# DRAM copies of q and k in pieces of 512 columns, fewer W2 splits in the last key blocks, first casts on two engines

## The chip, the cores and the metric

The kernel runs on one core of one Trainium2 chip. The metric is the device time of one execution, in microseconds (us). The engines are TensorE (PE), VectorE (DVE), ScalarE (ACT), GpSimd (POOL) and SyncE (SP), whose only work here is to issue DMAs.

## What is computed

For x of 2048 tokens by 512 features, all in float32:

```python
g = sigmoid((x * gate_w).sum(-1))                 # one gate for a token
qkv = x @ wqkv                                    # 32 heads of 16
scores = q @ k.T / 4, for keys within the last 256 tokens, causal
a = (softmax(scores) @ v) @ wo
y = layernorm(x)
b = gelu(y @ w1 + b1) @ w2 + b2                   # 512 -> 1792 -> 512
out = g * a + (1 - g) * b
```

## The kernel before, in words

Float32 products are made of fp32r parts: an operand is cast to a high part (`copy` on ACT, or a copy on DVE) and the rest is a low part (`lo_part`, a subtraction on DVE or POOL); three matmuls, high by high, high by low and low by high, stand for one. `split(w, raw)` makes both parts of a weight tile; with `both=True` DVE makes the high part too.

The work has three stages, and the order of the instructions on each engine is written by hand (manual schedule). A step counter helps: `after(k, fn)` puts work off to the k-th `tick()` from now, and `settle()` runs the ticks until nothing is left.

**Stage 1, QKV** (to about 154 us). x comes in four chunks of 512 tokens (`load_x`), each in four pieces by feature. `qk_unit(g, t, c)` makes q or k (t) of eight heads (g) for one chunk with 12 matmuls (L233), and writes high and low parts to DRAM tiles `qkd[g, t]` of 50 rows for a head. `v_unit` makes v for 128 tokens (L254). Where group g is 0 the high part is written twice, into rows 0 and 1 + t; for g = 1, 2, 3 `double(g)` copies it later inside DRAM (L245). `masks()` sets constants on POOL.

**Stage 2, attention and MLP1** (154 to about 527 us). Heads are taken in groups of four, p = 0 to 7, and tokens in blocks of 128. The string ORDER says what PE does next:

- S: `s_pair`, scores of one query block by its key blocks for a pair of heads (L279); DVE masks and reduces them to row maxima (L288, L289). After four query blocks `put_max` sends the maxima through DRAM (`md`) into rows of the q stacks (L307, L309).
- T: `st_pair`, transposed scores of one key block, maximum included (L323); ACT takes the exponential (L325), POOL zeroes what lies outside the window with two affine selects (L327).
- P: `pv`, probabilities by v (L342), evacuated by ACT, or by DVE once no S is left (L349), and stored to `osc` (L353).
- f: `fill`, one of the 24 steps of an `mlp1_unit` (two matmuls of 64 rows side by side, L527). There are 28 units, so 672 steps. Their result goes to DRAM, tile `hp` (L539).

A T of a new key block first calls `block(p, kb)`, which ticks, and there the loads are issued: `load_stacks` (L266) for the next p, the copies of `double`, and in the last p the W2, Wo and h tiles of stage 3. S, T and P share four double PSUM banks in turn, of which an MLP1 unit holds one. S runs ahead of T by ten query blocks (LAG is 6). All DMAs but a few go through SP, which works in order; eight semaphores are shared in turn, so an issue waits until the DMA eight before it has landed. After ORDER come the last P and the MLP1 steps that are left.

**Stage 3, MLP2 with the output projection** (527 us to the end). `mlp2(c, f)` multiplies one h tile by one W2 tile, 12 matmuls (L724), for 14 f in each of four token chunks; h tiles are loaded four steps ahead (`load_h`, L579), put through gelu on ACT (L582) and split by DVE (L586). `attn_out(c)` normalises the attention output, splits it and multiplies it by Wo (L703).

The functions that the change touches:

Of the kernel before, what the change touches and what calls it, by code (L numbers as in the profile page):

```python
# [19 lines left out]
S = 2048  # L20
D = 512
H = 32
DH = 16
F = 1792
DT = D // 128
KT = D // 64
FT = F // 128
C = 512
# [6 lines left out]
EPS = 1e-5  # L35
NEG = -3.0e38
U8 = mybir.dt.uint8
ORDER = ("fSfTffSPffTfSffTfSffTfTfffSfTffSffSfffSPSffTfSffTfSffTfffTSPSfSfTfffTfffTSfTfffSfSPSTfTSfTffffSTPSTf"
         "TffSffTfSffTPSfTfTfffSfTffSffSPSfTfffTfSfTfffSfTPTfSfTfffTfSfTffSffTSfffSPTSfTffSffTPTSffTfSfTfSffSP"
         "SfTfSffTfTfSTfffTfSfSfPTSffTfSfTfSffTPTSfTffSfTfSffTPTSfTffTffSfTffSffSPSfTSfffTfSffTfSffTfffSTPTSff"  # L40
         "TfSffTfSffffSfSPTffTfSffTfffSfTPSfTfSfffTfSffTfSffTffSffSPSTffSffTfTffSfTfffTffSPTfSfTffSfffTfSfffSP"
         "TfSfTffSfTffTfSPTfSfTffSffTfSffTfSffTffSffSPTSfTfffTfSPSffTfSffTfSffTffSffTfSffTffSffSPTSTfffSffTPTf"
         "SfTffSffTSffTfSffSPTfSfTffTfffSfSPSffTfSffTfSffTfSfffTSffTfffSTPSfTfSffTfSffSPTSfTffSffTfSffTfffTTPT"
         "fTfSffTfffTfSPTSfTffSffSPSfTSfffTfSffTffTfSfTfffTfSPSfTffSffTffSffSPTSfTfffTfSfTfffSfTPTSfTffSffTfSf"
         "fTfSffTfSffSPTSfTfffSfTfffTfSPTfSfTfffSffTfffSTPTSfTfffSfSPSffTffTfSffTffSffTfSffTfSffffSfTffSffSPSf"
         "TfffTfSfTffSffTPTfSfTffSfffTfSffTfSfffSPTfSffTfffTfSPTfSfTfffSfTffSffTfSffTffSffSPTSfTfffSfTPTfSfTff"
         "SffTfffSTPTfSffTfSffTfSfffSPTSffTfSfTfSffTfSffTSffSPTSffTfSffTffTfSfTffSfSPTfSfTffSffTTfffSPTfSffTfS"
         "ffTffTfSfffSfffSPTfSfTffSffTfSffTfSfffSPTfSfTffTffSfTfffSfSPTSTffffTSPTSfTfffTfSfTffTffSPTSfTffSffTS"
         "ffTfSffSPTSTfffSffTPTSfTffSffTSffTfSffSPSTfSTSTfTffTPTTffffTfPTfffTffTfffTffTPTffTffffTfTPTTfffffTTP"
         "TfT")  # L50
LAG = 6


# [1 line left out]
def gated_mix_kernel(ctx, tc: tile.TileContext, xt, x2, wqk, wv, wo, xa, gw, w1, w2, b1, b2, out):  # L55
# [55 lines left out]
    def view(t, *ap, off=0):  # L111
        return bass.AP(tensor=t.tensor, offset=t.offset + off, ap=[list(x) for x in ap])

    def f32(t):
        return t.bitcast(F32)

    def lo_part(lo, src, hi, eng=dve):
        eng.tensor_tensor(out=lo, in0=src, in1=f32(hi), op=ALU.subtract)  # L118

    def copy(dst, src):  # L120
        act.activation(dst, src, AF.Copy)  # L121
# [4 lines left out]
    def after(k, fn):  # L126
        todo.setdefault(step[0] + k, []).append(fn)
# [40 lines left out]
    def split(w, raw, both=False):  # L168
        if both:
            dve.tensor_copy(w[:, 0], raw)  # L170
        else:
            copy(w[:, 0], raw)
        lo_part(w[:, 1], raw, w[:, 0])

    def masks():
        for t in qs + ks:
            pool.memset(f32(t[:32]), 0.0)
        for k in ks:
            pool.memset(f32(k[96:128]), 1.0)
        one = small("scr", 2, (128, 256), BF16)  # L180
        pool.memset(one, 1.0)
        pool.affine_select(out=one[:, :128], in_=one[:, :128], pattern=[[-1, 128]], base=0, channel_multiplier=1,
                           compare_op=ALU.is_ge, fill=0.0)
# [24 lines left out]
    def load_x(c):  # L208
        h, l = x8(), x8()
        xh.append(h)  # L210
        xl.append(l)
        raw = vs[:, 4 * c:4 * c + 4].rearrange("p b r -> p (b r)")
        for dt in range(DT):
            sp.dma_start(raw[:, dt * C:(dt + 1) * C], xt[c, :, dt * C:(dt + 1) * C])

        def rest(first=None):
            for dt in range(DT):
                a, r = h[:, dt * C:(dt + 1) * C], raw[:, dt * C:(dt + 1) * C]
                copy(a, r)
# [19 lines left out]
            act.dma_start(f32(view(d, [S, DH], [50 * S, HG], [1, C], off=k * DH * S + c * C)), f32(h))  # L239
        after(1, lambda: sp.dma_start(f32(view(d, [S, DH], [50 * S, HG], [1, C], off=(2 - t) * DH * S + c * C)), f32(l)))  # L240

    def double(g):
        for t in range(2):
            fr, to = (f32(view(qkd[g, t], [S, DH], [50 * S, HG], [1, S], off=k * DH * S)) for k in (0, 1 + t))
            sp.dma_start(to, fr)  # L245

    def v_unit(b):
# [298 lines left out]
    def load_w2(f):  # L546
        if f % 2 == 0:
            w2t.append(x8())
            if f == 4:
                spare.append(x8())  # L550
        w = w2s[f] = w2t[-1][:, f % 2 * 2 * C:f % 2 * 2 * C + 2 * C].rearrange("p (k n) -> p k n", k=2)
        raw = t2()
        sp.dma_start(raw, w2[f])
        return lambda both=False: split(w, raw, both)
# [5 lines left out]
        return lambda both=False: split(w, raw, both)  # L560

    def early_w2():
        for n in range(3):
            def go(n=n):
                fns = [load_w2(2 * n), load_w2(2 * n + 1)]
                after(2, lambda: [fn(True) for fn in fns])
            after(1 + n, go)

        after(2, lambda: early_wo(0))

    def early_wo(a):
        fns = [load_wo(a), load_wo(a + 1)]
        after(3, lambda: [fn(True) for fn in fns])

    hs = {}

# [24 lines left out]
    def block(p, kb):  # L601
        tick()
        if kb % 2 == 0:
            if kb and p + 1 < 8:
                load_stacks(p + 1, kb * 128 - 256, 256)
            if not kb and p:
                load_stacks(p, S - 256, 256)
        if p in (0, 1, 3) and kb == 10:
            double((p + 3) // 2)
        if p == 7 and kb == LAG:  # L610
            early_w2()
        if p == 7 and kb == 13:
            early.extend(load_h(0, f) for f in range(4))

    early = []
# [188 lines left out]
```

## Time and profile before

| | |
|---|---|
| timed runs | 737.3 us median of 3 (733.98 to 737.37) |
| the profiled execution | 735.38 us |
| its span | 733.7 us, 16078 instructions |
| granted PE clock, mean | 0.998 |
| DMA | 138.45 MB, mean 189 GB/s |
| chain that ended last | PE 83%, DMA 6%, DVE 6%, issue 2%, ACT 1%, SP queue 1% |

The profile is of one execution. Groups of instructions give the number of them, the busy time and the mean of one. In a row of windows come the stretch, its length, and the busy time and count of PE, of its weight loads, of DVE, ACT and POOL, then PE's granted clock, the share of DMA time and GB/s. In a row of the timeline or of the chain the first number is the start and the second the duration; brackets hold the engine's idle time just before and what ended it. PE counts as busy from a matmul's start to its modelled end, so short stops between matmuls do not show as idle time. A row of the queue's waits has the sum, the number and the longest.

### The profile page before, as it was taken

Reading aid. Unit: us, or ns where it says so; the run is one execution under the profiler, and the core shown is the slowest. Engines: PE = TensorE matmul, PEld = TensorE weight load, DVE = VectorE, ACT = ScalarE, POOL = GpSimd, SP = SyncE. Lnnn points to the kernel's source line nnn. Section 1 sums busy time; section 2 is a strip of 40 time slices with the busy share of each in tenths; the row PEclk is TensorE's granted clock in tenths of the full one; section 3 lists DMA queues with packets and bytes.
Section 4 is the critical chain, followed back from the end, with each engine's and each line's share of the span. In section 5 each row is a group of like instructions: output and inputs, shape, how many; then the busy total and the mean of one; then the engine's idle time right before and its main releaser. Section 6 shows DMA issues by size and latency. Waiting matters only on the chain.

```text
span 733.7 us, 16078 instructions
## 1 busy us (share of the span) xinstructions
PE 709.5 (97%) x5728; PEld 538.7 (73%) x5728; DVE 494.8 (67%) x1049; ACT 367.7 (50%) x576; POOL 271.2 (37%) x548
## 2 busy tenths in 40 slices
PE   6999999999999899999999999999999999999997
PEld 4677777776766577777777777766678788888886
DVE  4438885778787677887778778786465645735544
ACT  4432122457667467666776767767433323223221
POOL 9220007759656355554664546547300000000000
PEclk9999999999999999999999999999999999999999
DMA  8999757776745765548664553625475544442541
GB/s 322 316 284 320 210 156 244 238 214 213 239 147 167 244 204 185 177 136 251 216 188 164 184 165 126 200 92 176 153 238 174 167 138 137 150 136 94 189 135 57
DMA packets 101795, 138.45 MB, mean 189 GB/s; under 512 B 15348, under 2 KB 54708, under 8 KB 100820
## 3 DMA queue, kind: packets, MB, share of 16 engines
q1 hardware_dynamic: 95812, 126.68, 54.5%
q10 hardware_dynamic: 5904, 10.75, 4.6%
q8 instruction: 46, 0.75, 0.4%
q14 instruction: 33, 0.27, 0.1%
HBM read 82.06 MB, written 54.28 MB: 186 GB/s over the span
## 4 chain that ended last, share of the span: by engine, by line
PE 83%; DMA 6%; DVE 6%; issue 2%; ACT 1%; SPq 1%; ACTq 0%; POOL 0%; DVEq 0%
PE ps_a L724 20%; PE ps_b L527 18%; PE ps_b L342 10%; PE ps_d L233 10%; PE ps_b L323 7%; PE ps_o L703 6%; PE ps_b L279 6%; PE ps_d L254 5%; DVE mx L289 2%; DMA v<-in_xt 1%; DVE ps_b L288 1%; DMA q<-md 1%; DMA t<-in_wo 1%; DMA t<-in_wv 1%; PE ps_x L279 1%
## 5 line engine op out<-in xcount | busy, mean ns | idle before, releaser
L327 POOL TENSOR_SCALAR_AFFINE_SELECT p<-p 128x256 f32<-128x256 f32 x480 | 186.5, 418 | 144.7 <-ACT p L325 141.8
L527 PE MATMUL ps_b<-x,w 64*128 64x512 f32 x1344 | 222.9, 395 | 0.1
L325 ACT ACTIVATE p<-ps_b 128x768 f32<-128x768 f32 (+2 forms) x256 | 191.7, 771 | 59.5 <-PE ps_b L323 52.3
L724 PE MATMUL ps_a<-x,t 128*128 128x512 f32 x624 | 149.7, 397 | 0.5 <-DVE t L586 0.5
L289 DVE TENSOR_REDUCE mx<-ps_b 128x2 f32<-128x512 f32 x208 | 144.1, 693 | 7.2
L724 PEld LDWEIGHTS ps_a<-x,t 128*128 128x128 f32 x624 | 117.2, 188 | 30.2 <-DVE t L586 1.4
L527 PEld LDWEIGHTS ps_b<-x,w 64*128 64x128 f32 x1344 | 131.8, 186 | 9.3 <-DVE t L349 0.4
L288 DVE COPY_PREDICATED ps_b<-tri,ps_b 128x256 f32<-128x256 uint8 x208 | 88.3, 424 | 50.6 <-PE ps_b L279 42.4
L233 PE MATMUL ps_d<-x,w 128*128 128x512 f32 x384 | 98.3, 407 | 8.0 <-ACT w L121 6.7
L323 PE MATMUL ps_b<-q,k 64*128 64x384 f32 (+5 forms) x512 | 97.1, 365 | 6.3 <-DVE mx L289 2.3
L342 PE MATMUL ps_b<-p,v 128*32 128x128 f32 (+1 forms) x1920 | 93.3, 332 | 0.9 <-POOL p L327 0.7
L233 PEld LDWEIGHTS ps_d<-x,w 128*128 128x128 f32 x384 | 72.6, 192 | 29.0 <-ACT w L121 6.7
L279 PE MATMUL ps_b<-k,q 62*128 62x384 f32 (+2 forms) x472 | 88.0, 352 | 3.9 <-DMA k<-qk 2.2
L342 PEld LDWEIGHTS ps_b<-p,v 128*32 128x32 f32 x1920 | 54.4, 110 | 37.0 <-issue 6.9
L323 PEld LDWEIGHTS ps_b<-q,k 50*128 50x128 f32 (+1 forms) x512 | 52.0, 184 | 38.7 <-PE ps_b L279 15.3
L121 ACT ACTIVATE t<-ps_b 128x256 f32<-128x256 f32 (+1 forms) x114 | 52.6, 489 | 51.7 <-PE ps_b L342 43.5
L279 PEld LDWEIGHTS ps_b<-k,q 62*128 62x128 f32 x472 | 48.5, 184 | 22.6 <-ACT p L325 6.0
L582 ACT ACTIVATE t<-t,b1s 128x512 f32<-128x512 f32 x56 | 38.8, 718 | 48.6 <-DMA t<-hp 48.4
L118 DVE TENSOR_TENSOR t<-t,t 128x512 fp32r<-128x512 f32 x68 | 47.1, 693 | 14.0 <-ACT t L121 11.5
L416 POOL TENSOR_TENSOR t<-t,t 128x512 f32<-128x512 f32 x16 | 22.6, 1412 | 76.8 <-DMA qk<-t 73.1
L254 PE MATMUL ps_d<-wv,x 128*128 128x512 f32 x192 | 47.5, 396 | 0.5 <-ACT wv L121 0.5
L703 PE MATMUL ps_o<-w,t 128*128 128x512 f32 x192 | 46.4, 390 | 0.0
(73 smaller groups left out, 500.7 us busy)
## 6 DMA issues: line engine op xcount, KB each, us to landing
hp<-t SPq DMA_DIRECT2D x56, 256.0 KB
t<-hp SPq DMA_DIRECT2D x56, 256.0 KB
k<-qk SPq DMA_DIRECT2D x112, 98.0 KB
q<-qk SPq DMA_DIRECT2D x112, 98.0 KB
qk<-t ACTq DMA_DIRECT2D x40, 256.0 KB
qk<-t SPq DMA_DIRECT2D x32, 256.0 KB
osc<-t SPq DMA_DIRECT2D x32, 256.0 KB
t<-in_w SPq DMA_DIRECT2D x28, 256.0 KB
```

What stands on the lines that cost most here:

```text
L233: pe.matmul(o, a[:, dt * 128:(dt + 1) * 128], b[:, dt * C:(dt + 1) * C], start=n == 0, stop=n == 11)
L254: pe.matmul(o, x[:, a:a + 128], wvs[dt][:, k], start=n == 0, stop=n == 11)
L279: pe.matmul(o[:, e, :n], qs[pr][r:k, qb * 128:qb * 128 + 128], ks[pr][r:k, t0:t0 + n], start=True, stop=True)
L288: dve.copy_predicated(o[:, :, :128], tri, o[:, :, 256:384])
L289: dve.tensor_reduce(m, o[:, :, :256], mybir.AxisListType.X, ALU.max)
L323: pe.matmul(o[:, e, :w], ks[pr][r:k, kb * 128:kb * 128 + 128], qs[pr][r:k, kb * 128:kb * 128 + w], start=True, stop=True)
L325: act.activation(pt[:, :, :w], o[:, :, :w], AF.Exp, scale=0.25)
L327: pool.affine_select(out=pt[:, :, a:a + 128], in_=pt[:, :, a:a + 128], pattern=[[0, 2], [sgn, 128]], base=b, channel_multiplier=-sgn, comp ...
L342: pe.matmul(a[32 * h:32 * h + 32, at:at + w], vs[:, kb, v:v + 32], pts[p, kb][:, h, fr:fr + w], start=n == 0, stop=n == len(parts) - 1, sk ...
L527: pe.matmul(o[:, e], w[kt // 4][r:r + 64, k, m:m + 128], y[r:r + 64, a:a + C], start=n == 0, stop=n == 23)
L703: pe.matmul(a, x[:, g], wos[g][:, k], start=n == 0, stop=n == 11)
L724: pe.matmul(accs[c][b], x[:, b * 128:(b + 1) * 128], w, start=f == 0 and n == 0, stop=f == FT - 1 and n == 2)
```

## The change

It does these things:

- The copies of `double` are made in pieces of 512 columns: two copies of 256 KB at each of key blocks 9, 11, 13 and 15 of p = 0, 1 and 3, where two copies of 1 MB stood at key block 10.
- In p = 7 four W2 tiles (one in each of four blocks) and not six W2 and two Wo tiles are loaded and split. W2 tiles 4 and 5 follow in MLP2's first steps. The Wo tiles are loaded in MLP2's first and third step and split four ticks later, with the high part on ACT and not on DVE.
- The first four h tiles are loaded at key block 12 of p = 7, not 13.
- The high part of the first weight tile is made ahead of that of the first x chunk; in the first chunk pieces 0 and 2 are cast by DVE, 1 and 3 by ACT; the low part of piece 3 is made by POOL. In all chunks the high parts are put ahead of the low parts. The clearing of 32 rows of each stack is put ahead of these casts on POOL; it was the first work of `masks()`.
- ORDER is another string: the same number of S (236), T (256) and P (64), and 655 f in place of 647, with 17 MLP1 steps left behind it in place of 25. The f are 96, 81, 80, 96, 88, 87, 86 and 41 in the eight p, after 89 (two ahead of the first T), 73, 95, 80, 85, 92, 81 and 52.

```diff
--- before.py
+++ after.py
@@ -35,19 +35,19 @@
 EPS = 1e-5
 NEG = -3.0e38
 U8 = mybir.dt.uint8
-ORDER = ("fSfTffSPffTfSffTfSffTfTfffSfTffSffSfffSPSffTfSffTfSffTfffTS
...
-         "TfT")
+ORDER = ("TSPTffffTSfTffSfSPTfSTffSfffTfSfTSffTfSfTSfSfffSPfSfTfTffff
...
+         "fTfffTPTffT")
 LAG = 6
 
 
@@ -173,8 +173,6 @@
         lo_part(w[:, 1], raw, w[:, 0])
 
     def masks():
-        for t in qs + ks:
-            pool.memset(f32(t[:32]), 0.0)
         for k in ks:
             pool.memset(f32(k[96:128]), 1.0)
         one = small("scr", 2, (128, 256), BF16)
@@ -197,6 +195,8 @@
         w, raw = wt(), t2()
         wq[g, t] = w
         (eng or sp).dma_start(raw, wqk[g, t])
+        if eng:
+            return lambda: copy(w[:, 0], raw), lambda: lo_part(w[:, 1], raw, w[:, 0])
         return lambda: split(w, raw)
 
     def load_wv(dt):
@@ -213,13 +213,16 @@
         for dt in range(DT):
             sp.dma_start(raw[:, dt * C:(dt + 1) * C], xt[c, :, dt * C:(dt + 1) * C])
 
-        def rest(first=None):
+        def part(t, dt):
+            return t[:, dt * C:(dt + 1) * C]
+
+        def rest(hi=copy, first=None):
             for dt in range(DT):
-                a, r = h[:, dt * C:(dt + 1) * C], raw[:, dt * C:(dt + 1) * C]
-                copy(a, r)
-                lo_part(l[:, dt * C:(dt + 1) * C], r, a, dve if c < 3 else pool)
-                if dt == 0 and first:
-                    first()
+                (hi if dt % 2 == 0 else copy)(part(h, dt), part(raw, dt))
+            if first:
+                first()
+            for dt in range(DT):
+                lo_part(part(l, dt), part(raw, dt), part(h, dt), dve if c and c < 3 or not c and dt < 3 else pool)
 
         return rest
 
@@ -239,9 +242,9 @@
             act.dma_start(f32(view(d, [S, DH], [50 * S, HG], [1, C], off=k * DH * S + c * C)), f32(h))
         after(1, lambda: sp.dma_start(f32(view(d, [S, DH], [50 * S, HG], [1, C], off=(2 - t) * DH * S + c * C)), f32(l)))
 
-    def double(g):
+    def double(g, c):
         for t in range(2):
-            fr, to = (f32(view(qkd[g, t], [S, DH], [50 * S, HG], [1, S], off=k * DH * S)) for k in (0, 1 + t))
+            fr, to = (f32(view(qkd[g, t], [S, DH], [50 * S, HG], [1, C], off=k * DH * S + c * C)) for k in (0, 1 + t))
             sp.dma_start(to, fr)
 
     def v_unit(b):
@@ -451,7 +454,10 @@
     x1, x2nd = load_x(1), load_x(2)
     wvr = [load_wv(dt) for dt in range(DT)]
     x3 = load_x(3)
-    x0(w0)
+    for t in qs + ks:
+        pool.memset(f32(t[:32]), 0.0)
+    w0[0]()
+    x0(dve.tensor_copy, w0[1])
     w1st()
     x1()
     masks()
@@ -546,7 +552,7 @@
     def load_w2(f):
         if f % 2 == 0:
             w2t.append(x8())
-            if f == 4:
+            if f == 2:
                 spare.append(x8())
         w = w2s[f] = w2t[-1][:, f % 2 * 2 * C:f % 2 * 2 * C + 2 * C].rearrange("p (k n) -> p k n", k=2)
         raw = t2()
@@ -560,17 +566,15 @@
         return lambda both=False: split(w, raw, both)
 
     def early_w2():
-        for n in range(3):
+        for n in range(4):
             def go(n=n):
-                fns = [load_w2(2 * n), load_w2(2 * n + 1)]
-                after(2, lambda: [fn(True) for fn in fns])
+                fn = load_w2(n)
+                after(2, lambda: fn(True))
             after(1 + n, go)
-
-        after(2, lambda: early_wo(0))
 
     def early_wo(a):
         fns = [load_wo(a), load_wo(a + 1)]
-        after(3, lambda: [fn(True) for fn in fns])
+        after(4, lambda: [fn() for fn in fns])
 
     hs = {}
 
@@ -605,11 +609,11 @@
                 load_stacks(p + 1, kb * 128 - 256, 256)
             if not kb and p:
                 load_stacks(p, S - 256, 256)
-        if p in (0, 1, 3) and kb == 10:
-            double((p + 3) // 2)
+        if p in (0, 1, 3) and kb >= NB // 2 and kb % 2:
+            double((p + 3) // 2, kb // 2 - 4)
         if p == 7 and kb == LAG:
             early_w2()
-        if p == 7 and kb == 13:
+        if p == 7 and kb == 12:
             early.extend(load_h(0, f) for f in range(4))
 
     early = []
@@ -666,7 +670,8 @@
     b2s = get("work", "b2s", 1, (128, D))
     sp.dma_start(b2s, view(b2, [0, 128], [1, D]))
 
-    early_wo(2)
+    for n in range(2):
+        after(1 + 2 * n, lambda n=n: early_wo(2 * n))
     us = {}
 
     def attn_out(c):
@@ -740,7 +745,7 @@
         for k in (n + 4,):
             c, f = item(k)
             if f >= 0:
-                if c == 0 and f > 5:
+                if c == 0 and f > 3:
                     waiting["w", f] = load_w2(f)
                 waiting[c, f] = load_h(c, f)
         c, f = item(n + 1)
```

More of the change, by code (lines that the diff above doesn't have):

```diff
@@ L37 @@
 U8 = mybir.dt.uint8
[L38 to L49, printed above, removed]
-         "TfT")
@@ new lines @@
+ORDER = ("TSPTffffTSfTffSfSPTfSTffSfffTfSfTSffTfSfTSfSfffSPfSfTfTffffTSfTfffSfSPSffTTfffSfTffTffSffSPSffTfTfff"
+         "ffSffTffSffSPSfTfSfffTfTffSfffffSffTfffTfSPTfSfTffSffSPTSffTffTfSfTffSfSPTfSfTffTffSfTfffTfSfTffSffS"
+         "PSffTSffTffTffSPTSffTffSfTffSffTPTfSffTfSffTfSffTfSffTfffSPTSTSTSPSTfSfffTffSffTfSffffTSPTfSfTfffTfS"
+         "fTffSffSPTfSffTffTfSfffTPSfTffTffSfTfffTfSfTffSffSPTSfTfffSfTffSffTPTfSfTfffSfTPSTfTfffSfTffSffSPSfT"
+         "SfffTSfffTfSfTfTffSPTSfffTSfTffTfSfTffSffSPTfSffTfSffTffTffSPTfSfTffSfffTffSfTffSffSPSfTfTfffSfTffSf"
+         "fTPTfSfTffSfffTfSffTffSffSPTfSfTffSffTfTfffSPSfTSfffTSfffTfSffTffSffSPSfTffTffSfTfffTfSPTfSfTffSffTf"
+         "fSffTfSfffSPTfSfTffTfffSPSfTfTfffSfTffSffTfSffTffSffSPTSfTfffTfSPTSfffTfSffTfSfTfSffSPTSffTffTSffTff"
+         "SPTfSfTfffTfSffTfSffTffSffSPTfSfTffSfffTffSPSTffSffTfSffTfSfffSPSfTffSffTfTffSffTfffSTPSTffTffSfTffS"
+         "ffSPTfSfTfffSfTffTffSfTfffSfSPSTfSfffTfSffTfSffTfffTSPTfSffTfSffTfSffTSffSPTfSfTffSffTffSffTPTfSfTff"
+         "TffSPTfSTfffTffSffSPTfSfTffSffTfSffTfTffSfTfffSfSPSffTfSfTfSffSPSTffTffSfTfffTfSfTffTffSPSfTfSfffTfS"
+         "fTfSffSPTfSfTffTfffSfTPSffTffSfTffSffTfSffTfSfffSPTSTfffSffTfSffTfffSTPSfTSfffTfSffTfSfffTffSPSTfSff"
+         "fTfSffTfTfSPTSfTfffSfTPTSfTffTffSfTffSffSPSTTSTSSTTPTSffTfffTTPTffTfffTfTPTTffTfffTPTfTTffffffTfPTTf"
+         "fTfffTPTffT")
```

## The prediction

> **What bounds the kernel now.** I read the page first, then the windows by stage, then the chain of waits and the timeline of TensorE around its gaps, then the queue's own waits.
>
> ```profile
> PE 709.5 (97%) x5728; PEld 538.7 (73%) x5728; DVE 494.8 (67%) x1049; ACT 367.7 (50%) x576; POOL 271.2 (37%) x548
> L289 DVE TENSOR_REDUCE mx<-ps_b 128x2 f32<-128x512 f32 x208 | 144.1, 693 | 7.2
> L288 DVE COPY_PREDICATED ps_b<-tri,ps_b 128x256 f32<-128x256 uint8 x208 | 88.3, 424 | 50.6 <-PE ps_b L279 42.4
> ```
>
> TensorE is in use for 97% of the span, so the change can gain only where PE stands still, runs at a low clock, or is held up between two short matmuls. It issues the same matmuls before and after: the letters T, S and P are the same in number in both orders, and the 672 MLP1 steps are only divided otherwise (647 in the order and 25 behind it, then 655 and 17). So I look for the places of loss.
>
> ```profile
> 154.00:203.00 49.00, 45.63 (x514) 33.69 (x514) 41.27 (x90) 33.83 (x54) 34.52 (x69) 1.00 0.71 221
> 346.00:390.00 44.00, 43.91 (x508) 33.05 (x510) 34.10 (x82) 31.45 (x48) 25.25 (x62) 1.00 0.62 190
> 481.00:521.00 40.00, 37.38 (x474) 25.14 (x470) 29.25 (x57) 26.37 (x39) 27.49 (x61) 1.00 0.42 144
> 540.00:728.00 188.00, 188.00 (x808) 151.42 (x806) 103.01 (x174) 57.53 (x90) 0.00 (x0) 1.00 0.43 138
> 253.40:257.20 3.80, 3.77 (x38) 2.19 (x40) 1.12 (x2) 1.33 (x3) 1.34 (x3) 0.55 0.46 117
> ```
>
> The first number after the stretch is its length, the second PE's busy time. From 540 to 728 us PE never rests, and from 346 to 390 it rests 0.09 us: nothing is to be had there. It rests 3.4 us at the start of attention, 2.6 us in the last head group, and in one place (253.4 to 257.2) it is busy at a granted clock of 0.55. Those, the first 40 us and the seam to MLP2 are the places where this change can act.
>
> **Prices.** From the chain of waits, back to back pieces of PE:
>
> ```profile
> 346.92 0.70 PE ps_b L527 x6
> 346.56 0.18 PE ps_b L323 x2
> 231.90 1.44 PE ps_b L342 x32
> ```
>
> So an f step (two matmuls of L527) takes 0.235 us, a T pair 0.18 us (an S pair I price alike) and a P 1.44 us. An S pair costs DVE 0.424 + 0.693 = 1.12 us.
>
> **The DRAM copies.** Before, heads' groups p = 0, 1 and 3 each issue two copies of 1 MB at key block 10. What the one in p = 1 does (first the chain, then PE's timeline, then a row of the queue's waits):
>
> ```profile
> 236.87 0.61 SPq L245
> 239.44 9.34 DMA q<-md
> 253.93 2.72 PE ps_b L342 x32
> 256.65 0.59 PE ps_b L323 x2
> ```
>
> ```profile
> 248.92 0.54 PE L323 MATMUL ps_b<-q,k 64*128 64x384 f32 x2 [0.57 <-DMA q<-md]
> 253.43 0.50 PE L279 MATMUL ps_b<-k,q 62*128 62x384 f32 x2 [2.22 <-DMA k<-qk]
> ...
> SPq L266 <- DMA qk<-qk: 13.5, 6, 2.9
> ```
>
> The copies go out at 236.87; the maxima's rows (q<-md), issued behind them at 239.44, land 9.34 us later, and the stack loads of L266 wait six times for a copy to land, 13.5 us in all: six waits for six copies. PE pays 0.57 + 2.22 us of rest, and then one P takes 2.72 instead of 1.44 us and one T pair 0.59 instead of 0.18, the low clock of the table above. Sum 0.57 + 2.22 + 1.28 + 0.41 = **4.5 us**. In p = 0 and p = 3 the same queueing costs PE nothing that I can tell: the S pairs there come later than the loads, and that lead is the cover.
>
> After, each of the three p issues eight copies of 256 KB, two at each of key blocks 9, 11, 13 and 15. SP issues 24 instead of 6: at 0.61 us each 11 us more on SP, which is spread over twelve blocks of about 2.8 us (44 us for 16 of them in the second window above). How long a 256 KB transfer keeps the queue is seen where SP waits for one landing after another:
>
> ```profile
> 536.19 0.33 SPq L553 DMA_DIRECT2D t<-in_w  x1
> 536.82 0.32 SPq L579 DMA_DIRECT2D t<-hp  x1
> 537.49 2.89 SPq L675 DMA_DIRECT2D su<-osc  x4
> ```
>
> These three issues wait for the landings of three 256 KB loads in turn: 0.63 and 0.67 us apart. A copy inside DRAM reads and writes there, so I take up to twice that, 1.3 us. Two pieces then put a load behind them back by 1.3 to 2.6 us, against the 9.34 us above. I take the whole 4.5 us as gained (0 if something else in that place is late next, which is a rival below).
>
> The rule against this edit: the Trainium skill, DMA: Bandwidth & Descriptors, section Bandwidth, says to batch DMAs to at least 1 MiB, and prices one DMA at about 2.0 us fixed plus its bytes. By that, estimated, four pieces cost 6 us more than one copy of 1 MB, and 36 us of queue over the six copies. The landings 0.67 us apart in the rows above do not bear it out for transfers in flight together. The sum goes by the rows.
>
> **The last key blocks and the splits.** Before, six W2 tiles and two Wo tiles are split on DVE alone between 505 and 516 us. The groups of that stretch, one row of the quiet stretch 346 to 390, and PE's gaps:
>
> ```profile
> L327 POOL TENSOR_SCALAR_AFFINE_SELECT p<-p 128x256 f32<-128x256 f32 x26 | 14.5, 597 | 1.4 <-ACT p L325 1.4
> L118 DVE TENSOR_TENSOR x<-t,x 128x512 fp32r<-128x512 f32 x6 | 4.6, 771 | 0.2
> L170 DVE CAST x<-t 128x512 fp32r<-128x512 f32 x6 | 3.5, 590 | 0.7 <-DMA t<-in_w 0.7
> ```
>
> ```profile
> L327 POOL TENSOR_SCALAR_AFFINE_SELECT p<-p 128x256 f32<-128x256 f32 x60 | 22.8, 408 | 20.1 <-ACT p L325 19.6
> ```
>
> ```profile
> 505.33 13.70 POOL L327 TENSOR_SCALAR_AFFINE_SELECT p<-p 128x256 f32<-128x256 f32 x24 [1.05 <-ACT p L325]
> 513.86 0.41 PE L342 MATMUL ps_b<-p,v 128*32 128x128 f32 x4 [0.71 <-POOL p L327]
> 516.64 0.50 PE L323 MATMUL ps_b<-q,k 64*128 64x256 f32 x4 [0.64 <-DVE t L349]
> ```
>
> While DVE splits, a POOL select takes 597 instead of 408 ns, and POOL works 13.7 us without a rest, so it has become the engine that the last P wait for: 26 x 0.189 = 4.9 us of POOL time. PE's visible price is 0.71 + 0.64 = 1.35 us. After, four splits (4 x 1.36 = 5.4 us of DVE, one in each block) stand for eight (10.9 us). Half of the 4.9 goes, **2.5 us**; bounds 1.35 and 4.9. The cover for the moved work is MLP2, where DVE is busy 103 of 188 us and ACT 58.
>
> **The seam to MLP2.** Two W2 splits and two Wo splits more stand in MLP2's first steps, and each transfer moved with them counts.
>
> ```profile
> 526.45 2.59 SPq L539 DMA_DIRECT2D hp<-t  x4
> 530.67 0.90 SPq L579 DMA_DIRECT2D t<-hp  x2
> 537.50 1.48 ACT L582 ACTIVATE t<-t,b1s 128x512 f32<-128x512 f32 x2 [8.82 <-DMA t<-hp]
> 538.86 6.38 PE L724 MATMUL ps_a<-x,t 128*128 128x512 f32 x25 [0.49 <-DVE t L586]
> 540.24 0.62 ACT L121 ACTIVATE x<-t 128x512 fp32r<-128x512 f32 x1
> 540.89 0.69 DVE L118 TENSOR_TENSOR x<-t,x 128x512 fp32r<-128x512 f32 x1 [0.29 <-ACT x L121]
> ```
>
> The h tile of f = 4 lands at 537.5 and PE already waits 0.49 us for its cast. Ahead of it in SP's queue four hp stores, b2s and two Wo loads have gone. After, 17 and not 25 steps are left behind the order, so the last but one MLP1 unit (24 steps each) ends inside it and two of the four stores go earlier: minus 2 x 0.67. The load of W2 tile 4 now stands in front of the h tile: plus 0.67. On ACT and DVE the new split of W2 tile 4 stands between the gelu and the cast: plus 0.62 + 0.69. For f = 5 two Wo splits (1.38 us on DVE) and one W2 split stand in line against a step of about 2.8 us of PE: another 0.5 us. Sum **+1.1 us**; from -0.5 (stores gone, all else covered) to +3.
>
> **The first casts.** ACT casts the weights first, DVE two of the four x pieces, POOL takes one low part.
>
> ```profile
> 6.73 13.71 PE L233 MATMUL ps_d<-x,w 128*128 128x512 f32 x48 [6.73 <-ACT w L121]
> 20.90 6.74 PE L233 MATMUL ps_d<-x,w 128*128 128x512 f32 x24 [0.45 <-ACT x L121]
> 37.64 3.31 PE L233 MATMUL ps_d<-x,w 128*128 128x512 f32 x13 [0.73 <-POOL x L118]
> ...
> 14.32 5.23 DMA v<-in_xt
> ```
>
> PE might start up to 0.6 us sooner (one ACT cast), but it stops again at 20.90 and 37.64 for x tiles that the loads set (the last row, of the chain, lands at 19.55 whatever PE does). So the edit is worth **0**; a later start of up to 0.45 us is hidden by the same gap, and I give it -0.6 to +0.6.
>
> **The order.** Counted from the strings with the prices above: two S pairs stand closer than DVE's 1.12 us in 119 places before (short by 29 us in all) and 101 after (31 us), so the bulk is equal. But the new order has two long stretches without an f: in p = 1 SPTSTSTSPST, where DVE needs 5 x 1.12 = 5.6 us against 5 x 0.18 + 4 x 0.18 + 2 x 1.44 = 4.5 on PE, and in p = 7 SPSTTSTSSTTPTS, 6.7 against 5.0. The longest before has five letters. That is 2.8 us at most; the PSUM banks let PE run ahead, so I take half, **+1.4 us** (0 to 2.8).
>
> **Sum.** The profiled execution took 735.38 us (span 733.7 and 1.7 around it); the three timed runs lie from 733.98 to 737.37 with a median of 737.3, so it stands inside them, 1.9 under the median. 735.4 - 4.5 - 2.5 + 1.1 + 0 + 1.4 = **730.9 us**, 0.6% less.
>
> **Rivals.** (A) Slower, 739.4: the pieces make the stack loads late. The smallest PE work between a stack load's place in the order and its first S pair falls from 7.3 us to 5.5 (then 5.7, 6.8, 6.9, all in p = 1 and p = 2, three of them behind the pieces of key blocks 11 to 15). The four loads of a block take SP some 2 us, and one more until the last lands: about 3.5. If a pair of pieces puts them back by 4.1 us, the four waits are 2.1 + 1.9 + 0.8 + 0.7 = 5.5, and two lower clocks at 1.5 each make 8.5. It decides from a delay of about 2 us on; my bounds are 1.3 to 2.6, which is why it is not small. The skill's rule above leads here. (B) No change, 735.4: the place at 249 to 253 us stays late, since q<-md, two weight swaps and two sets of stack loads meet there without any copy; then 4.5 us are not gained. Against it: SP's waits there name the copies. (C) More, 725: the tail gives its 4.9, the stretches cost nothing, and the early order removes 2 of the 3.4 us at 154 to 203: 735.4 - 4.5 - 4.9 + 1.1 - 2.
>
> **Chances.** Forecast (727 to 734) 0.40, A 0.22, B 0.23, C 0.15. About 0.5%, 3.7 us, is what a measurement of this kernel can tell from no change: the line runs at 731.7, close to the forecast itself. Of the forecast's 0.40 some 0.33 lies with the faster side by its likely surplus over the two penalties, which are bounds more than readings, and 0.07 with no change. Faster 0.33 + 0.15 = 0.48, same 0.07 + 0.23 = 0.30, slower 0.22. The forecast's own range is 727 to 734; the range for all reaches to C and A: 723 to 741.
>
> **What would show it.** Right: no PE gap on q<-md or k<-qk near 250 us and a granted clock of 1.00 there; SP waits on qk<-qk short; POOL's selects in the last blocks near 500 ns and no PE gap for POOL; PE's gap at the fifth MLP2 step 1 to 2 us. Wrong: PE gaps on k<-qk in p = 1 or 2 (A); the same gap with another name at 250 us (B); a gap over 3 us at MLP2's start.

## The result, and the profile after

The kernel after takes 737.6 us (median of 20 runs, 735.65 to 739.54) against 735.2 (median of 20, 733.09 to 738.27): ratio 1.0029, 95% interval 1.0016 to 1.0042. It is 0.3% slower, where 0.6% faster was forecast: the size is within the 0.5% that the forecast took for no change, but the interval lies wholly on the slower side, so the direction was wrong. The profiled execution took 738.54 us (span 736.8, mean granted PE clock 0.999).

The page of the profile after, engine line and the MLP1 matmuls; then the windows of before again, now of the kernel after (the stretches are the same, the work in them has moved by a few us):

```profile
PE 709.2 (96%) x5728; PEld 538.8 (73%) x5728; DVE 492.7 (67%) x1044; ACT 369.9 (50%) x580; POOL 273.0 (37%) x549
L533 PE MATMUL ps_b<-x,w 64*128 64x512 f32 x1344 | 221.0, 395 | 1.3 <-DVE mx L292 1.3
```

```profile
154.00:203.00 49.00, 46.52 (x503) 33.71 (x506) 42.08 (x93) 32.70 (x50) 33.91 (x66) 1.00 0.66 203
346.00:390.00 44.00, 42.63 (x508) 32.40 (x508) 35.13 (x83) 29.82 (x45) 24.27 (x59) 1.00 0.60 187
481.00:521.00 40.00, 36.08 (x458) 24.63 (x458) 24.20 (x48) 28.85 (x44) 26.35 (x64) 1.00 0.44 146
540.00:728.00 188.00, 186.79 (x796) 149.24 (x797) 107.21 (x182) 60.69 (x96) 0.00 (x0) 1.00 0.46 145
253.40:257.20 3.80, 3.80 (x56) 2.58 (x52) 2.02 (x4) 2.10 (x4) 0.79 (x3) 1.00 0.74 220
```

The place that the copies had cost is clean: from 253.4 to 257.2 PE issues 56 matmuls instead of 38, at clock 1.00 instead of 0.55. But the stretch from 346 to 390, where before PE rested 0.09 us, now has 1.37 us of rest, and over the kernel the MLP1 matmuls wait 1.3 us for a PSUM bank that DVE is reading (0.1 us in all before). The last head group rests 3.92 us (40.00 less 36.08) instead of 2.62.

PE's timeline at the new gaps, and the instructions around the largest:

```profile
216.26 0.44 PE L282 MATMUL ps_b<-k,q 62*128 62x384 f32 x2 [1.23 <-DMA q<-qk]
265.16 0.44 PE L282 MATMUL ps_b<-k,q 62*128 62x384 f32 x2 [0.63 <-DMA q<-qk]
514.34 0.44 PE L326 MATMUL ps_b<-q,k 64*128 64x384 f32 x2 [1.70 <-DVE t L352]
540.84 17.36 PE L729 MATMUL ps_a<-x,t 128*128 128x512 f32 x72 [1.21 <-DVE t L590]
```

```profile
511.83 0.77 DVE L118 TENSOR_TENSOR x<-t,x 128x512 fp32r<-128x512 f32 x1
512.53 0.62 DVE L170 CAST x<-t 128x512 fp32r<-128x512 f32 x1
513.18 0.77 DVE L118 TENSOR_TENSOR x<-t,x 128x512 fp32r<-128x512 f32 x1
513.88 0.41 DVE L352 COPY t<-ps_b 128x256 f32<-128x256 f32 x1
```

Two stack loads come late in p = 1 and p = 2 (1.23 and 0.63 us). At 514.34 a T waits 1.70 us for the bank of a P: DVE empties that bank (L352), but stands behind two weight splits first. The last row of PE's timeline is the seam, 1.21 us.

SP's own waits, and the selects of the last key blocks (groups from 505 to 523 us):

```profile
SPq L310 <- DMA qk<-qk: 3.9, 5, 1.6
SPq L269 <- DMA qk<-qk: 1.3, 2, 1.0
```

```profile
L330 POOL TENSOR_SCALAR_AFFINE_SELECT p<-p 128x256 f32<-128x256 f32 x31 | 13.9, 490 | 4.3 <-ACT p L328 4.3
```

The 13.5 us in which stack loads waited for copies are 1.3, and a select takes 490 instead of 597 ns. So the parts that the forecast had counted as gains are there; the loss is elsewhere.

**Where the time is, by stretch.** A PE gap is only part of it, since matmuls that stand close hold each other up. For each stretch from the first T of one p to the next I took its length less its matmuls at undisturbed prices (0.235 us for an f, 0.176 for a T or S pair of 384 columns, 1.44 for a P, 2.80 for an MLP2 step, 2.73 for 12 matmuls of Wo). Loss in us, from the profiled execution of each kernel ("D+S+W" has every part of the change but the order and is described below):

| | p0 | p1 | p2 | p3 | p4 | p5 | p6 | p7 and the f left | MLP2 to first Wo | rest |
|---|---|---|---|---|---|---|---|---|---|---|
| before | 8.0 | 7.3 | 7.9 | 3.9 | 3.8 | 3.4 | 4.8 | 7.7 | 1.1 | 5.1 |
| after | 8.4 | 5.9 | 5.6 | 3.5 | 5.8 | 5.0 | 4.4 | 7.7 | 1.8 | 6.3 |
| D+S+W | 8.0 | 6.1 | 4.2 | 3.9 | 4.8 | 3.4 | 4.8 | 5.4 | 1.3 | 7.8 |

After against before: 3.7 us won in p1 and p2, where the copies were; 3.7 lost in p4 and p5, where the order differs and, at p4's start only, the pieces of p = 3; nothing won in the tail; 1.9 lost in MLP2. The start of attention, 156.0 against 154.4, is not in the table: it scatters from execution to execution (below).

The two long stretches of letters without an f that the forecast had priced stand in p1 and p7. SPTSTSTSPST takes 6.13 us (from 232.38) for 4.46 us of matmuls, SPSTTSTSSTTPTS 7.21 us (from 493.58) for 4.99: 1.7 and 2.2 us over their work. In the second, PE stops four times for banks that DVE's reductions hold:

```profile
495.70 0.44 PE L326 MATMUL ps_b<-q,k 64*128 64x384 f32 x2 [0.34 <-DVE mx L292]
496.77 0.44 PE L326 MATMUL ps_b<-q,k 64*128 64x384 f32 x2 [0.45 <-DVE mx L292]
497.83 0.73 PE L326 MATMUL ps_b<-q,k 64*128 64x384 f32 x4 [0.27 <-DVE mx L292]
498.89 1.51 PE L345 MATMUL ps_b<-p,v 128*32 128x256 f32 x32 [0.34 <-DVE mx L292]
```

### The profile page after: what moved, and what is told of

It is laid out like the page before. It is cut to its first block, busy times and chain, and to the rows that moved or that the text cites. A ratio compares the mean times of both kernels' runs of the same rounds, so it can differ in the third digit from the quotient of the medians.

```text
span 736.8 us, 16115 instructions
## 1 busy us (share of the span) xinstructions
PE 709.2 (96%) x5728; PEld 538.8 (73%) x5728; DVE 492.7 (67%) x1044; ACT 369.9 (50%) x580; POOL 273.0 (37%) x549
## 4 chain that ended last, share of the span: by engine, by line
PE 83%; DMA 6%; DVE 5%; issue 3%; POOL 1%; ACT 1%; SPq 1%; POOLq 0%; ACTq 0%; DVEq 0%
PE ps_a L729 19%; PE ps_b L533 19%; PE ps_b L345 11%; PE ps_d L236 10%; PE ps_b L326 6%; PE ps_b L282 6%; PE ps_o L708 6%; PE ps_d L257 5%; DVE mx L292 2%; DVE ps_b L291 1%; DMA t<-hp 1%; DMA q<-qk 1%; DMA t<-in_wv 1%; PE ps_x L282 1%; DMA v<-in_xt 1%
## 5 line engine op out<-in xcount | busy, mean ns | idle before, releaser
L236 PE MATMUL ps_d<-x,w 128*128 128x512 f32 x384 | 99.9, 410 | 8.9 <-DVE x L221 7.2
L326 PE MATMUL ps_b<-q,k 50*128 50x384 f32 (+5 forms) x512 | 95.5, 358 | 6.0 <-DVE mx L292 1.8
L345 PE MATMUL ps_b<-p,v 128*32 128x128 f32 (+1 forms) x1920 | 91.3, 329 | 1.0 <-DVE mx L292 0.5
L282 PEld LDWEIGHTS ps_b<-k,q 62*128 62x128 f32 (+1 forms) x472 | 48.3, 184 | 28.2 <-issue 8.1
```

Of the source, the lines that this page charges most:

```text
L236: pe.matmul(o, a[:, dt * 128:(dt + 1) * 128], b[:, dt * C:(dt + 1) * C], start=n == 0, stop=n == 11)
L282: pe.matmul(o[:, e, :n], qs[pr][r:k, qb * 128:qb * 128 + 128], ks[pr][r:k, t0:t0 + n], start=True, stop=True)
L326: pe.matmul(o[:, e, :w], ks[pr][r:k, kb * 128:kb * 128 + 128], qs[pr][r:k, kb * 128:kb * 128 + w], start=True, stop=True)
L345: pe.matmul(a[32 * h:32 * h + 32, at:at + w], vs[:, kb, v:v + 32], pts[p, kb][:, h, fr:fr + w], start=n == 0, stop=n == len(parts) - 1, sk ...
```

## The experiments

The change falls into four parts: **D**, the pieces of `double`; **S**, the first casts and the clearing of the stacks; **W**, the W2, Wo and h tiles; **O**, the order. My theory once the result was known was that the order costs what the other parts win; the rivals were late stack loads behind the pieces (A), the seam, and a later start of attention. Ratios are to the kernel before, on the same chip.

**One part alone, in the kernel before.**

```diff
# D                                   # O
-  if ... and kb == 10:               -ORDER = ("fSfTffSPff...
-      double((p + 3) // 2)           +ORDER = ("TSPTffffTS...
+  if ... and kb >= NB // 2 and kb % 2:
+      double((p + 3) // 2, kb // 2 - 4)
# S: load_wqk, load_x, masks, first casts   # W: load_w2, early_w2, early_wo, h tiles
```

> The kernel before with the copies in pieces of 512 columns alone. Theory (the copies' gain is real, other parts take it back): 3.5 to 4.5 us faster than before, no PE gap on q<-md or k<-qk near 250 us, granted clock 1.00 there. Rival (the new order made that gap go, or the place stays late without the copies): within 1 us of before.

> The kernel before with the new ORDER alone. Theory: 2 to 4 us slower than before, most of it in p = 4 to 6, where after spends 3.3 us more over its own work than before; the stall of the 1 MB copies stays. Rival (the losses of p = 4 to 6 come from the pieces' extra DMA issues on SP): within 1 us of before.

> The kernel before with the new first casts and the stacks' clearing ahead of them alone. Theory (VectorE's casts of SBUF tiles wait for POOL's memsets and the lost time is not caught up in QKV): 1.3 to 2.0 us slower, attention starts near 156.0 us, not 154.4. Rival (the loads set that stage anyway, as predicted): within 0.5 us of before.

> The kernel before with the moved W2, Wo and h loads and splits alone. Theory: the last head group gains 1 to 2 us from the lighter VectorE and POOL, and MLP2's first 50 us lose 1.8 us: 0 to 1 us slower. Rival (the prediction's tail): 2.5 us gained there and 1.1 lost at the seam, 1.4 us faster.

| | ratio | interval | median, us |
|---|---|---|---|
| D | 0.9945 | 0.9925 to 0.9965 | 731.9 |
| O | 1.0047 | 1.0030 to 1.0064 | 738.8 |
| S | 0.9987 | 0.9972 to 1.0003 | 735.7 |
| W | 1.0012 | 0.9997 to 1.0027 | 737.3 |

D is 0.55% faster, 4.0 us (735.2 x 0.0055), O 0.47% slower, 3.5 us; S and W cannot be told from 1. (Before has a median of 736.4 us among these runs, and among those of the next table; by the medians D wins 4.5 us and O loses 2.4.) The windows of D from 240 to 260 us, and its queue's waits:

```profile
240.00:260.00 20.00, 19.70 (x222) 14.94 (x218) 16.92 (x36) 13.12 (x21) 10.52 (x25) 1.00 0.79 238
```

```profile
SPq L307 <- DMA qk<-qk: 1.4, 1, 1.4
SPq L266 <- DMA qk<-qk: 0.9, 2, 0.6
```

The same stretch of before:

```profile
240.00:260.00 20.00, 17.15 (x174) 12.26 (x170) 12.31 (x26) 9.66 (x16) 7.51 (x18) 0.91 0.75 229
```

What the pieces leave is a wait for the maxima (q<-md) at p4's start, behind the pieces of p = 3: 0.7 us in D and 1.1 in D+S, none in the run below that has the same order and no copies.

In W's profile the tail loses 5.6 instead of 7.7 us, and POOL's selects fall to 481 ns. But from MLP2's start to its fifth step it takes 12.5 us, where before takes 11.9 and the other kernels without W 11.2, and from the first to the second chunk's Wo product it takes 46.6 instead of 45.15: the attention output's copy on ACT comes late there, as in this row of D+S+W (below), which has it worst. What the tail gives, MLP2 takes.

```profile
569.47 2.79 PE L708 MATMUL ps_o<-w,t 128*128 128x512 f32 x11 [1.30 <-ACT t L121]
```

**The parts together.**

> The kernel before with the pieces and the new ORDER. The pieces alone gave 0.9945 and the order alone 1.0047. Theory (the two are not additive: under the new order the S pairs follow their stack loads so closely that q<-qk is late with the pieces too): p = 1 and p = 2 together gain under 1.5 us over the order alone, 737 to 739 us, ratio 1.001 to 1.005. Rival (additive): 0.9992, and 4 us less in p = 1 and p = 2.

> The kernel after with the old ORDER (copies, first casts and splits as after). Theory (the order is what turns the change's gain round): ratio to before 0.993 to 0.996, 5 to 7 us under after, its tail loss near the 5.6 us of the run with the splits alone, not the 7.7 of after. Rival (the seam to MLP2 and the start take it back): 0.999 to 1.002.

> The kernel before with the pieces and the first casts, no other part. Theory (both act in their own places): ratio 0.993 to 0.995, the fastest so far together with the pieces alone. Rival (the casts' contention with POOL's memsets costs what the first run of after showed at the start): 0.996 to 0.998, attention from 156 us on.

| | ratio | interval | median, us |
|---|---|---|---|
| O+D | 1.0051 | 1.0033 to 1.0069 | 739.5 |
| D+S+W (after, with the old order) | 0.9948 | 0.9934 to 0.9962 | 732.4 |
| D+S | 0.9935 | 0.9923 to 0.9947 | 731.8 |

D+S+W against after differ in the order alone: 0.9948 and 1.0029, 0.8% or 5.9 us. D+S has the lowest ratio, 0.65% faster than before; it beats before and after, but cannot be told from D or D+S+W, whose intervals overlap with its own.

And D is worth 4 us with the old order and nothing with the new one (1.0051 against O's 1.0047). The profiles show where. p1 and p2 lose 15.3 us in before and 10.4 in D, but 12.2 in O and 11.9 in O+D. With the new order and no pieces, the place of before's stall has one gap of 2.18 us, after which the clock stays at 1.00; with pieces the stack loads and maxima are late:

```profile
252.98 0.44 PE L279 MATMUL ps_b<-k,q 62*128 62x384 f32 x2 [2.18 <-DMA q<-qk]
```

```profile
214.81 0.44 PE L279 MATMUL ps_b<-k,q 62*128 62x384 f32 x2 [0.44 <-DMA q<-qk]
270.64 0.53 PE L323 MATMUL ps_b<-q,k 64*128 64x384 f32 x2 [1.28 <-DMA q<-md]
```

(the first fence is O, the second O+D.) The profiled O is the slowest of its ten runs, 743.1 against a median of 738.8, so I take the places from it and the sizes from the ratios. It loses 3.8 us more than before in p4 to p6, as I had expected, but also 5.5 more in the tail (13.2 against 7.7; O+D 11.0). Its largest gap is there, a wait for DVE's bank, here behind four W2 splits in a row (512.8 to 518.9 us):

```profile
519.30 0.69 PE L323 MATMUL ps_b<-q,k 64*128 64x384 f32 x2 [3.65 <-DVE t L349]
```

So W, which is worth nothing under the old order, may be worth something under the new one: from O+D to after, which has S and W besides, the tail's loss falls from 11.0 to 7.7 us, MLP2 takes 2.1 of it back, and the ratio goes from 1.0051 to 1.0029, with intervals that overlap.

**The clock.** With some of its gaps PE falls to half its granted clock for a few us (in the profile of O from 500.6 to 503.9 and from 517.6 to 524.4). At half clock a P took 2.72 instead of 1.44 us in before, so such a stretch costs at most half of its length, which is also what it takes from the mean clock of the run. This mean is on record for every run: O's ten have 0.9942, before's 27 among them 0.9970. The difference, 0.0028 of 737 us, gives an estimate of up to 2.1 us of O's loss. Between after (0.9987) and D+S+W (0.9997) it is 0.7 of 5.9 us at most, so there the order costs by its waits and its close matmuls.

**The bank that DVE empties in the tail.** Let ACT empty it, in the kernel after, and in the best version:

```diff
-                    pv(*a, not ls)
+                    pv(*a, False)
```

> The kernel after with the last P evacuated by ACT and not by VectorE (the argument of pv that says so is always false). Theory (in the new order's last blocks T waits for a bank that VectorE empties late, behind two W2 splits): the 1.70 us gap at 514 us goes, 1 to 2 us faster than after. Rival (ACT, with an exponential of 0.81 us for each T, is the engine that holds the tail): the gap stays with ACT's name, 0 to 1.5 us slower than after.

> The pieces and the first casts under the old order, with the last P evacuated by ACT as in the earlier run. Theory (VectorE's splits stand in front of the copy in the old order too, 0.6 to 1.5 us of PE in the last blocks): 0.5 to 1.5 us faster than the pieces with the first casts, ratio 0.991 to 0.9935. Rival (MLP2's fifth step waits for loads that start at a time PE does not set): the gain comes back as a longer gap there, ratio 0.993 to 0.995.

After with it: 1.0019 (1.0000 to 1.0038), against 1.0029 for after; the two intervals overlap. The gap of 1.70 us goes and p7 loses 5.6 instead of 7.7 us, but MLP2's fifth step now waits longer:

```profile
540.50 1.01 PE L729 MATMUL ps_a<-x,t 128*128 128x512 f32 x2 [2.67 <-DVE t L590]
```

It starts at 540.5, where after started at 540.8: SP issues the last hp stores 1.8 us sooner (527.2 for 529.0), but the gelu of this h tile starts only 0.3 sooner (538.05 for 538.39), so its loads and its cast set that time and not what PE has saved before. In the best version the edit was a miss: 0.9985 (0.9964 to 1.0007) against 0.9935, 0.5% or 3.7 us lost. By the mean clock of the runs (0.9957 against 0.9992) up to 2.6 us of that is low clock, by the same estimate. There ACT's copies of the last P stand behind four gelus (2.56 us) and the load of their table (1.28 us), and an f step waits for the bank. Its profile also has a longer wait for the maxima at p4's start, 1.70 us instead of the 1.10 of D+S, which I can't put down to the edit:

```profile
347.89 0.60 PE L326 MATMUL ps_b<-q,k 64*128 64x384 f32 x2 [1.70 <-DMA q<-md]
522.26 1.22 PE L533 MATMUL ps_b<-x,w 64*128 64x512 f32 x4 [2.74 <-ACT t L121]
```

**No copies at all.** Every group's high parts are stored twice in stage 1, as for g = 0, and `double` is not called (S is in both; one has the old order, one the new):

```diff
-        for k in (0, 1 + t)[:1 + (g == 0)]:
+        for k in (0, 1 + t):
```

> The old order and the new first casts, and no copies at all: qk_unit writes the high part twice for every group, 24 more stores of 256 KB on ACT's queue in QKV. Theory (the 1 MB copies were the whole stall in p = 1 and 2): like the pieces with the first casts, ratio 0.992 to 0.995; the 0.7 to 1.1 us wait on q<-md at the start of p = 4, which the pieces left, goes. Rival (QKV has no room for 6 MB more): attention starts more than 2 us later than 154 to 156 us and the ratio is over 0.997.

> The same without copies under the new ORDER. Theory (the new order itself lets S and T follow their loads too closely, whatever the copies do): p = 1 and 2 together still lose 11 us or more over their own work, ratio 1.002 to 1.006. Rival (under the new order it is the pieces that are late): p = 1 and 2 lose 10 us or less, as under the old order with pieces, ratio 0.998 to 1.001.

Old order 0.9993 (0.9978 to 1.0007), new order 1.0071 (1.0058 to 1.0084); both theories had put the ratio lower. With the 6 MB of stores p0 loses 12.9 and 13.1 us instead of 8.0 and 8.4 (both profiles have 6.8 us at half clock there, from 161.4 and 159.2 us on), so neither is a version to keep. Nor is all of the difference between the two ratios the order's waits: the runs' mean clock is 0.9944 and 0.9902, up to 3.1 of 5.7 us. But they tell the order apart from the copies where the clock is at 1.00. In p1 and p2 the two lose the same, 10.05 (6.31 + 3.74) and 10.06 (5.60 + 4.46), while with pieces it is 10.3 (D+S) and 11.5 (after). So in p1 and p2 the new order is not bad in itself, though I had thought it was: the 1.2 us between D+S and after are late loads behind the pieces, which is rival A in small. In p4 and p5 the new order loses 10.9 (5.84 + 5.01) against 6.9 (3.56 + 3.36) with no copy anywhere: that is its own.

**The stretches without an f.** 16 of the 17 that have three or more letters in p = 4 and 5 of the new order, broken by one f from the nearest longer run (the two long ones of p1 and p7 stay as they are):

```diff
-...ffSffSPTSfTfffTfSPTSfffTfSff...
+...ffSfSPfTSfTfffTfSPfTSffTfSff...
```

> The kernel after, with the letters of p = 4 and 5 alone moved: 16 stretches of three or more letters without f are broken by one f from the longer neighbouring run, all counts kept. Theory (there PE waits for PSUM banks that VectorE empties after clustered S pairs): p = 4 and 5 lose 8 us over their work and not 10.8, 2 to 3 us faster than after. Rival (the losses come from elsewhere in those groups, such as the loads): within 0.7 us of after.

1.0087 (1.0068 to 1.0106): 0.6% worse than after. p4 and p5 lose 14.9 instead of 10.8 us. The waits there, after first (from 346 to 443 us), then broken (347 to 449):

```profile
ACT t L121 <- PE ps_b L345: 16.6, 16, 2.5
PE ps_b L533 <- DVE mx L292: 1.0, 2, 0.6
PE ps_b L282 <- DVE mx L292: 0.8, 2, 0.6
```

```profile
ACT t L121 <- PE ps_b L345: 23.6, 16, 2.5
PE ps_b L326 <- ACT t L121: 1.6, 4, 0.4
```

With an f put between P and T, four T come to wait for a bank which ACT has not emptied yet (1.6 us of the 4.1), and ACT waits 7 us longer for the P. So the short stretches were not the cost of p4 and p5; my theory of them fell. It says nothing of the two long ones, which no run changed by themselves.

**Halves of the orders.** After, with the letters of p = 4 to 7 from the old order; and the other way round (one S and one P of the seam adjusted, so that each letter's number is kept):

```diff
-ORDER = new p0-p3 + new p4-p7
+ORDER = new p0-p3 + "SP" + old p4-p7
+ORDER = old p0-p3 + new p4-p7 less its first S and P
```

> The kernel after with the letters of p = 4 to 7 from the old ORDER (SP put in between so that the counts agree; 9 MLP1 steps are left behind the order, not 17). Theory (the order costs by its own letters, mostly in p = 4, 5 and 7): p = 4 and 5 lose about 8 us over their work and not 10.8, p = 7 with what follows 5.5 and not 7.7; ratio 0.996 to 0.999. Rival (the state handed over from the first half, such as where an MLP1 unit ends, makes the loss): p = 4 and 5 stay at 10 us or more.

> The kernel after with the letters of p = 0 to 3 from the old ORDER (33 MLP1 steps left). Theory: p = 4 and 5 lose 10 to 11 us, p = 7 with what follows 7 to 8, p = 1 and 2 together 10.3 as under the old order; ratio 0.999 to 1.002. Rival: p = 4 and 5 fall to 9 us or less.

New then old 1.0072 (1.0051 to 1.0093), old then new 1.0120 (1.0102 to 1.0137): both slower than either whole order. p4 + p5 lose 12.7 with the old letters behind the new first half (8.2 in D+S+W, the same letters behind the old one), and 15.9 with the new letters behind the old half (10.8 in after). Letters do not carry their cost with them. What differs is where in a run of letters an MLP1 unit ends: a unit holds one of the four bank pairs for 24 f, wherever these fall. Counted from the strings, at p4's first T a unit has done 1 of its 24 steps in the old order and 17 in the new; with the halves exchanged the old letters meet it at 17 and the new ones at 1.

**The phase alone.** D+S, the best version, with 8 or 24 f put ahead of p3's first T (and as many fewer left behind the order):

> The pieces and the first casts under the old order, with 8 f put in ahead of p = 3 (8 fewer stay behind the order). No other letter moves, but every MLP1 unit after that ends 8 f later against the T, S and P. Theory (where a unit takes and gives back its PSUM bank decides how long the same letters wait): p = 4, 5 and 6 lose 15 us or more over their work, where the pieces with the first casts lose 13.0. Rival (the letters alone decide): within 0.7 us of 13.0.

> The same with 24 f put in, a whole MLP1 unit, so that units end against the letters as before. Theory: p = 4, 5 and 6 lose 13.0 us, within 0.7, as without. Rival (any shift of the MLP1 work against the attention costs, for instance by its loads and stores): 15 us or more, as with 8.

Eight: 1.0075 (1.0058 to 1.0091). Twenty-four, a whole unit: 0.9967 (0.9951 to 0.9983), against 0.9935 for none. p4 to p6 lose 13.1 us without, 19.9 with 8 and 13.6 with 24. From the first T of p4 to that of p6, the windows of D+S, of 8 and of 24:

```profile
343.10:434.00 90.90, 89.48 (x1058) 68.22 (x1054) 70.11 (x167) 63.81 (x97) 50.65 (x124) 1.00 0.60 186
346.60:441.60 95.00, 92.61 (x1058) 67.78 (x1054) 70.93 (x167) 62.49 (x97) 50.43 (x124) 1.00 0.56 172
347.70:439.20 91.50, 89.83 (x1058) 68.40 (x1055) 70.61 (x167) 63.15 (x96) 49.18 (x123) 1.00 0.59 183
```

The same 1058 matmuls in the same sequence of letters take 90.9, 95.0 and 91.5 us: 4.1 us for a shift of a third of a unit, 0.6 for a whole one, all at a granted clock of 1.00. (The rest of what the 24 cost is mostly behind p6: with one MLP1 step left behind the order and not 25, p7 loses 9.4 instead of 7.5 us, 3.4 us of it at half clock from 500.6 on.) So these letters are worth what they are only at one place of the units. That it is the bank that the unit holds, and not its copy on ACT or its store, is not shown.

**The clearing of the stacks.** D+S with the loop of memsets behind the first casts, where POOL had it before:

```diff
-    for t in qs + ks:
-        pool.memset(f32(t[:32]), 0.0)
     w0[0]()
     x0(dve.tensor_copy, w0[1])
     w1st()
     x1()
+    for t in qs + ks:
+        pool.memset(f32(t[:32]), 0.0)
```

> The pieces and the first casts under the old order, with the clearing of the stacks behind the first casts on POOL. Theory (the two VectorE casts, 1.01 and 1.49 us in the profile of after, wait for POOL's memsets; the loads then hide it): casts of 0.4 to 0.5 us, PE's gap at 8.4 us gone, attention from 154 to 156 us as before, ratio within 0.1% of the pieces with the first casts (0.9935). Rival (the lost time is not hidden): 0.7 to 1.5 us faster than that, attention from 154 us or sooner.

0.9948 (0.9932 to 0.9965), D+S 0.9935: no difference that can be told. DVE's first casts, after, then with the memsets late:

```profile
5.35 1.01 DVE L221 CAST x<-v 128x512 fp32r<-128x512 f32 x1 [5.35 <-DMA v<-in_xt]
6.89 1.49 DVE L221 CAST x<-v 128x512 fp32r<-128x512 f32 x1 [0.53 <-DMA v<-in_xt]
```

```profile
5.18 0.43 DVE L221 CAST x<-v 128x512 fp32r<-128x512 f32 x1 [5.18 <-DMA v<-in_xt]
6.59 0.43 DVE L221 CAST x<-v 128x512 fp32r<-128x512 f32 x1 [0.98 <-DMA v<-in_xt]
21.86 1.55 PE L236 MATMUL ps_d<-x,w 128*128 128x512 f32 x3 [1.93 <-ACT x L121]
```

The casts take 0.43 us without the memsets beside them and up to 1.49 with them, and PE starts 0.5 us sooner (6.04 for 6.51); but at 21.86 it stops for the cast of an x tile, for whose load ACT has waited 2.31 us, and nothing is left of it. After that gap the clock is at half for 3.4 us, and attention starts at 157.0 here. Over the profiles of this case it starts between 154.0 and 157.0, with old and new casts alike, about 155.0 in the mean, so the 1.7 us between the first two profiles were scatter and no cost of S.

## Why the prediction was wrong, point by point

- **The failed step is the order's term**: "so the bulk is equal", +1.4 us with bounds of 0 and 2.8. It measured 5.9 us with all other parts in (1.0029 against 0.9948), 3.5 alone (2.4 by the medians). The step priced letters one by one and counted how close they stand. Both halves of it failed. The two long stretches, halved because the banks let PE run ahead, lose 3.9 us over their work in after (1.7 and 2.2), more than the 2.8 that it had as the most; p1 as a whole still loses no more than in D+S+W (5.9 against 6.1), so of the two only that of p7 can show in the sum. And the bulk is not equal: after against D+S+W the new order loses 0.4 us more in p0, 1.2 in p1 and p2, 2.3 in p4 to p6 and 2.3 in the tail, and 0.4 less in p3. The shifted orders show that the same letters cost 4.1 us more or less by where the MLP1 units end, which this count of S pairs could not see.
- **The copies**, -4.5: right in mechanism, place and size with the old order, -4.0. Wrong under the new one, where O and O+D measure the same. I had added terms that are not additive: the order moved both the S pairs that the copies stalled and the loads that the pieces delay. The rule on batching (the Trainium skill, DMA: Bandwidth & Descriptors, section Bandwidth), by which pieces would cost, is not borne out in D (0.9945). Of the 4.5 us, 1.7 was the low clock of one execution: in the profiles of S and W, where the 1 MB copies stay, PE has one gap at this place, put down to ACT, and the clock after it is 1.00 (S, then W):

```profile
253.41 0.44 PE L282 MATMUL ps_b<-k,q 62*128 62x384 f32 x2 [3.35 <-ACT p L328]
255.16 0.44 PE L279 MATMUL ps_b<-k,q 62*128 62x384 f32 x2 [2.66 <-ACT p L325]
```

- **Rival A** (late stack loads) is there, at 216.3 and 265.2 us, in p = 1 and p = 2 as it said, but of the 5.5 us of waits and 3 of low clock that it had, waits of 1.23 and 0.63 us came, at a clock of 1.00, and p1 and p2 lose 1.2 us more than in D+S. Other executions pay more: with the same letters and pieces, the kernel with ACT emptying the bank waits 2.07 us at 216.4 and the broken order 1.65 at 264.8, each with 3.4 us at half clock behind it. Its sign for the whole was right, but mostly for another reason.
- **Rival B** (the place stays late without any copy) fell: without copies p1 and p2 lose 10.05 us, with 1 MB copies 15.2. **C** fell too: p0, with the 154 to 203 us in which it saw 2 us to gain, loses 8.4 instead of 8.0.
- **The splits**, -2.5: 2.1 in the tail with the old order (7.7 to 5.6), the selects at 481 and 490 ns as forecast. With the new order the gain is taken by the long stretch of p7 and the T at 514.3. The engine named for this place was POOL; what is late next is DVE's emptying of a bank behind the splits, which I did not see coming although its 0.64 us stood among the rows.
- **The seam**, +1.1: mis-sized. The gap at the fifth step is 1.21 us as forecast, but W adds 0.6 to 1.3 us up to there (12.5 against 11.9 and 11.2) and 1.4 (W) to 2.6 (D+S+W) more between the Wo products of the first and the second chunk, which I had not looked at: in all 2.0 to 2.7 in W's own profile. So W is worth nothing under the old order (1.0012).
- **The first casts**, 0: held (0.9987, interval with 1).

Still open is why the new order's own letters lose 2.7 us more in p4 and p5 than D+S+W, and 3.9 more without copies. The waits there are on banks that DVE reads, 0.2 to 0.6 us each, and most of the loss is not in gaps but in matmuls that follow each other late; which meeting of unit end, P and S does it was not settled. An order made anew for the timing of the pieces was not tried, so it is not shown that pieces and another order could not win together.

## What to carry to other kernels

An order of instructions written out by hand can be tuned to the moments at which buffers come free, as it was here; change anything that shifts a long-held buffer against it and measure it again, since here counting the letters told neither its cost nor its sign. Run the parts of a change alone and all but one together: here the one part that was forecast as a small correction ate all that the best part won. When a gap goes, look at what is set by a landing further on (MLP2's fifth step here), for a gain ahead of it ends there.

## What was not expected of the hardware

After some gaps of PE the granted clock fell to half for 3.4 us, which can cost up to 1.7 us more, as much as the smaller of these gaps: in the best version with ACT emptying the bank, after each of its gaps of 1.70 and 2.74 us (windows from shortly after their ends):

```profile
348.20:351.60 3.40, 3.40 (x22) 2.42 (x23) 0.69 (x2) 1.62 (x2) 1.36 (x4) 0.50 0.67 217
522.30:525.70 3.40, 3.40 (x16) 2.71 (x18) 2.12 (x5) 0.40 (x1) 0.00 (x0) 0.50 0.41 154
```

The same was seen after before's 0.57 + 2.22 us, but not after 3.35 us in S, 2.66 in W, 2.18 in O nor 1.70 in the kernel after; and in the run with 24 f put in it came behind two gaps of 0.47 and 0.45 us. So a gap's length alone does not decide; what does is not shown.

A cast on DVE took 1.01 and 1.49 us beside POOL's memsets and 0.43 without them. The Trainium skill (SBUF — State Buffer, section Who interferes with whom) says that VectorE and GpSimd share a pair of ports that one of them holds at a time; the four rows of casts above agree.
